# The product with W4 by Strassen's scheme on pairs of 512-token blocks, after all of W3's product

## The chip, the core and the metric

One core of a Trainium2 chip runs the whole program. The metric is the device time of one execution in microseconds (us), as the median of three runs. In the profile, PE is the matmul engine (TensorE), DVE VectorE, ACT ScalarE, POOL GpSimd, and SP the engine that here only issues DMAs. Each engine works through its own instructions in the order in which they stand, and waits at the head of that order.

## The reference

The kernel computes attention over chunks, then two feed-forward layers on 3072 tokens. Only the last one is touched here: x is 3072 x 512, W3 (`w_in`) 512 x 2048, W4 (`w_out`) 2048 x 512.

```python
def _moe2_ref(x, w_in, w_out):
    h = x @ w_in
    g = np.maximum(0.01 * h, h)
    return (g @ w_out).astype(np.float32)
```

The weights arrive in 64-bit floats and are decoded on the chip. Every float32 product is made of three matmuls: each operand is split into a rounded high half and the low rest, and high x high, high x low and low x high are added up in PSUM.

## The kernel before

The first part (attention and the first layer) works on tiles of 128 tokens and leaves x in DRAM (`x2d`) and W3 decoded and split in DRAM (`w3d`). The change leaves it alone. The last layer takes the tokens in six blocks of 512 (`b`) and the 2048 hidden units in 16 slices of 128 (`f`):

- `load_x(b)` fetches a block of x and splits it; `load_w3(f)` fetches a slice of W3, `load_w4(f)` fetches and decodes a slice of W4. Both weights then stay in SBUF.
- `g_unit(b, f, ...)` makes a slice of g, 128 units x 512 tokens, with 12 matmuls into the PSUM tile `gp` (lines 89 and 515 to 529). ACT and DVE turn it into `u`, then the halves `gh` (ACT or DVE) and `gl` (POOL, or DVE in block 0) are made for the next product.
- `o_unit(b, f, ...)` (lines 531 to 548) adds that slice's part of the output with 12 matmuls to four PSUM tiles `po`, one for each 128 tokens, the halves of g being the stationary operand. After the last slice the tiles are copied to `o` (two buffers) and written to `out` in whole rows of 512 floats.

`flush(3)` holds the output's product three slices behind g, so PE alternates: 12 matmuls of line 89, 12 of line 535, 96 times. A scheduler fixes the order on each engine when the program is built. Tiles in a pool with `bufs=n` take turns: the n+1st waits until the first one's readers are done. DMAs also take turns on eight semaphores (shown as DMAHW0 to 7 in the orders below), so at most eight are under way.

Of the kernel before, what the change touches and what calls it, by code (L numbers as in the profile page):

```python
# [9 lines left out]
F32 = mybir.dt.float32  # L10
# [13 lines left out]
LAG = 5  # L24
# [15 lines left out]
def tile_kernel(  # L40
# [33 lines left out]
    w3d = dram.tile([KF2, P, 2 * 512], F32, name="w3d")  # L74

# [390 lines left out]
    sb, sw3 = ExitStack(), ExitStack()  # L466
    w3p = sw3.enter_context(tc.tile_pool(name="w3p", bufs=1, side="right", reuse_waits="tile"))
    NF3 = 8
    w3hl = [w3p.tile([P, NF3, 2, KD, P], F32R, name="w3a")]
    ps_g = sw3.enter_context(tc.tile_pool(name="ps_g", bufs=4, space=PSUM, reuse_waits="tile"))  # L470

    dec2 = sw3.enter_context(tc.tile_pool(name="dec2", bufs=3, side="right", reuse_waits="tile"))

    def load_w3(f):
        w = w3hl[f // NF3][:, f % NF3].bitcast(F32)
        nc.sync.dma_start(out=w.rearrange("p h k f -> p (h k f)"), in_=w3d[f])

    x2e = w3p.tile([P, 2, KD, BT], F32R, name="x2e")
    def load_x(b):
        hl = x2o if b % 2 else x2e  # L480
# [19 lines left out]
    w4p = sb.enter_context(tc.tile_pool(name="w4p", bufs=1, reuse_waits="tile"))  # L500
    w4h = w4p.tile([P, KF2, DM], F32R, name="w4h")
    w4l = w4p.tile([P, KF2, DM], F32R, name="w4l")
    w3hl.append(w4p.tile([P, KF2 - NF3, 2, KD, P], F32R, name="w3b"))
    x2o = w4p.tile([P, 2, KD, BT], F32R, name="x2o")
    pb = sb.enter_context(tc.tile_pool(name="pb", bufs=2, reuse_waits="tile"))
    pg = sb.enter_context(tc.tile_pool(name="pg", bufs=4, reuse_waits="tile"))
    ps_o = sb.enter_context(tc.tile_pool(name="ps_o", bufs=1, space=PSUM, reuse_waits="tile"))

    def load_w4(f):
        decode(load_raw(w4[f * P : (f + 1) * P, :], dec2), w4h[:, f], w4l[:, f], dec2, sub=nc.vector)  # L510

    def g_unit(b, f, xh, xl):
        ps = ps_g.tile([P, BT], F32, name="gp")
        w = w3hl[f // NF3][:, f % NF3]
        wh, wl = w[:, 0], w[:, 1]
        mm3(ps, [((wh[:, kk], wl[:, kk]), (xh[:, kk], xl[:, kk])) for kk in range(KD)])
        u = pg.tile([P, BT], F32, name="u")
        nc.scalar.activation(u, ps, AF.Copy, scale=0.01)  # L518
        nc.vector.tensor_tensor(out=u, in0=ps, in1=u, op=ALU.max)  # L519
        gh = pg.tile([P, BT], F32R, name="gh")  # L520
        gl = pg.tile([P, BT], F32R, name="gl")
        if b == 0:
            nc.scalar.activation(gh, u, AF.Copy)
        else:
            nc.vector.tensor_copy(gh, u)  # L525
        (nc.vector if b == 0 else nc.gpsimd).tensor_tensor(  # L526
            out=gl, in0=u, in1=gh.bitcast(F32), op=ALU.subtract
        )
        return gh, gl

    def o_unit(b, f, gh, gl, po):
        for t in range(TB):
            ts_ = slice(t * P, (t + 1) * P)
            for n, (a, w) in enumerate(((gh, w4h), (gh, w4l), (gl, w4h))):
                nc.tensor.matmul(  # L535
                    po[t], a[:, ts_], w[:, f],
                    start=(f == 0 and n == 0), stop=(f == KF2 - 1 and n == 2),
                )
        if f == KF2 - 1:
            for t in range(TB):  # L540
                late = b == NBLK - 1
                o = pg.tile([P, DM], F32, name="u") if late and t >= 2 else pb.tile([P, DM], F32, name="o")
                od = out[b * BT + t * P : b * BT + (t + 1) * P, :]
                if t % 2:
                    nc.vector.tensor_copy(o, po[t])
                else:
                    nc.scalar.activation(o, po[t], AF.Copy)
# [76 lines left out]
```

## Time and profile before

| | us |
|---|---|
| median of 3 runs (lowest, highest) | 923.99 (921.79, 924.91) |
| profiled execution: span, first to last instruction | 919.1 |
| PE busy in the span | 887.1 (97%) |
| DVE, ACT, POOL busy | 450.9, 315.8, 172.8 |
| share of PE in the chain that ended last | 85% |

The profile shows the span of the profiled execution; a run's time has the launch around it as well, and the median is 4.9 us above this span. Busy time of PE counts matmuls that overlap only once.

### The profile page before, as it was taken

Reading aid. Unit: us, or ns where it says so; the run is one execution under the profiler, and the core shown is the slowest. Engines: PE = TensorE matmul, PEld = TensorE weight load, DVE = VectorE, ACT = ScalarE, POOL = GpSimd, SP = SyncE. Lnnn points to the kernel's source line nnn. Section 1 sums busy time; section 2 is a strip of 40 time slices with the busy share of each in tenths; the row PEclk is TensorE's granted clock in tenths of the full one; section 3 lists DMA queues with packets and bytes.
Section 4 is the critical chain, followed back from the end, with each engine's and each line's share of the span. In section 5 each row is a group of like instructions: output and inputs, shape, how many; then the busy total and the mean of one; then the engine's idle time right before and its main releaser. Section 6 shows DMA issues by size and latency. Waiting matters only on the chain.

```text
span 919.1 us, 13605 instructions
## 1 busy us (share of the span) xinstructions
PE 887.1 (97%) x5248; PEld 713.2 (78%) x5248; DVE 450.9 (49%) x888; ACT 315.8 (34%) x830; POOL 172.8 (19%) x153
## 2 busy tenths in 40 slices
PE   3889999999999989999999999999999999999998
PEld 2467777777777768888888888888888888888886
DVE  4789976676787778389822112211321122112221
ACT  2578854455555555255421112111211121111111
POOL 2233310000000000000022224222422242222221
PEclk9999999999999999999999999999999999999999
DMA  9756785777888764787211001100200110001001
GB/s 230 192 163 185 191 253 172 222 238 201 262 241 251 219 195 172 295 297 267 69 46 46 1 1 46 46 1 1 88 4 1 46 47 1 0 1 46 1 1 46
DMA packets 51504, 109.94 MB, mean 120 GB/s; under 512 B 6640, under 2 KB 23024, under 8 KB 50672
## 3 DMA queue, kind: packets, MB, share of 16 engines
q1 hardware_dynamic: 38480, 93.87, 33.6%
q10 hardware_dynamic: 12960, 15.21, 5.4%
q8 instruction: 41, 0.67, 0.3%
q14 instruction: 23, 0.19, 0.1%
HBM read 79.70 MB, written 29.36 MB: 119 GB/s over the span
## 4 chain that ended last, share of the span: by engine, by line
PE 85%; DVE 7%; DMA 3%; ACT 2%; POOL 1%; issue 1%; SPq 0%; ACTq 0%; DVEq 0%; POOLq 0%
PE po L535 28%; PE gp L89 28%; PE x2p L345 14%; PE h L89 9%; DMA raw<-in_w 2%; PE att L240 2%; PE att L198 1%; DVE so L284 1%; PE tr L254 1%; PE tr L228 1%; ACT p L215 1%; POOL rstd L292 1%; DVE hnm L276 1%; DVE m L122 1%; DVE nms L207 1%
## 5 line engine op out<-in xcount | busy, mean ns | idle before, releaser
L519 DVE TENSOR_TENSOR u<-gp,u 128x512 f32<-128x512 f32 x96 | 66.3, 690 | 324.7 <-ACT u L518 324.7
L518 ACT ACTIVATE u<-gp 128x512 f32<-128x512 f32 x96 | 57.1, 594 | 354.3 <-PE gp L89 354.3
L526 POOL TENSOR_TENSOR gl<-u,gh 128x512 fp32r<-128x512 f32 x80 | 103.2, 1291 | 303.6 <-DVE gh L525 281.7
L535 PE MATMUL po<-w4h,gl 128*128 128x512 f32 x384 | 149.6, 390 | 0.0
L535 PE MATMUL po<-w4l,gh 128*128 128x512 f32 x384 | 149.6, 389 | 0.0
L535 PE MATMUL po<-w4h,gh 128*128 128x512 f32 x384 | 149.5, 389 | 0.0
L345 PE MATMUL x2p<-lhl,w2h 128*128 128x512 f32 x384 | 126.3, 405 | 3.0 <-ACT lhl L333 2.8
L345 PEld LDWEIGHTS x2p<-lhl,w2h 128*128 128x128 f32 x384 | 70.4, 189 | 19.8 <-ACT lhl L333 3.2
L535 PEld LDWEIGHTS po<-w4l,gh 128*128 128x128 f32 x384 | 72.1, 188 | 14.9
L535 PEld LDWEIGHTS po<-w4h,gl 128*128 128x128 f32 x384 | 72.1, 188 | 14.9
L535 PEld LDWEIGHTS po<-w4h,gh 128*128 128x128 f32 x384 | 72.1, 188 | 14.9
L345 PE MATMUL x2p<-lhl,w2l 128*128 128x512 f32 x192 | 77.7, 404 | 0.0
L89 PE MATMUL h<-w1l,xh 128*128 128x512 f32 x168 | 68.0, 405 | 1.9 <-POOL w1l L130 1.9
L89 PE MATMUL h<-w1h,xh 128*128 128x512 f32 x168 | 69.3, 412 | 0.5 <-ACT w1h L129 0.5
L89 PE MATMUL gp<-x2o,w3b 128*128 128x512 f32 x288 | 69.2, 390 | 0.0
L89 PE MATMUL gp<-x2o,w3a 128*128 128x512 f32 x288 | 69.2, 389 | 0.0
L89 PE MATMUL gp<-x2e,w3b 128*128 128x512 f32 x288 | 69.2, 390 | 0.0
L89 PE MATMUL gp<-x2e,w3a 128*128 128x512 f32 x288 | 68.7, 389 | 0.0
L89 PE MATMUL h<-w1h,xl 128*128 128x512 f32 x168 | 66.9, 398 | 0.0
L215 ACT ACTIVATE p<-att,nms 128x64 f32<-128x64 f32 x192 | 57.2, 319 | 22.1 <-DVE nms L208 21.9
L292 POOL TENSOR_TENSOR rstd<-ve,mhalf 128x1 f32<-128x1 f32 x24 | 15.8, 660 | 254.3 <-DVE ve L290 201.6
L89 PEld LDWEIGHTS gp<-x2o,w3b 128*128 128x128 f32 x288 | 54.1, 188 | 11.2
(107 smaller groups left out, 1261.3 us busy)
## 6 DMA issues: line engine op xcount, KB each, us to landing
raw<-in_w SPq DMA_DIRECT2D x48, 512.0 KB, 5.1
kbd<-in_kw SPq DMA_DIRECT2D x46, 256.0 KB, 4.5
vbd<-in_vw SPq DMA_DIRECT2D x46, 256.0 KB, 4.5
lnd<-sl SPq DMA_DIRECT2D x16, 512.0 KB, 3.7
lt<-lnd ACTq DMA_DIRECT2D x64, 128.0 KB, 4.5
q<-in_qt SPq DMA_DIRECT2D x24, 256.0 KB, 4.8
x2d<-x2s ACTq DMA_DIRECT2D x24, 256.0 KB, 3.8
out<-o SPq DMA_DIRECT2D x21, 256.0 KB, 2.0
```

The lines of the kernel that those rows point to most:

```text
L89: nc.tensor.matmul(ps, a, b, start=(i == 0), stop=(i == 3 * n - 1))
L122: nc.vector.scalar_tensor_tensor(out=mu, in0=raw[:, :, 1], scalar=0x80000000, in1=mu, op0=ALU.bitwise_and, op1=ALU.bitwise_or,)
L198: nc.tensor.matmul(sc[cs, 2 * hp : 2 * hp + 2, :], q[:, hp, cs], k[:, :, hp, c, :], start=True, stop=True,)
L207: nc.vector.tensor_reduce(out=nms, in_=sc, op=ALU.max, axis=AX.X, negate=True)
L215: nc.scalar.activation(p[:, h], sc[:, h], AF.Exp, bias=nms[:, h : h + 1], scale=SCALE, accum_out=rs[:, h : h + 1],)
L240: nc.tensor.matmul(xp[cs, 2 * hp : 2 * hp + 2, :], pt[:, hp, cs], v[:, :, hp, c, :], start=True, stop=True,)
L292: nc.gpsimd.tensor_tensor(out=rstd, in0=ve, in1=mhalf, op=ALU.pow)
L345: nc.tensor.matmul(ps, a[:, kk, es], r[:, kk], start=(kk == 0 and n == 0), stop=(kk == KF - 1 and n == 2),)
L518: nc.scalar.activation(u, ps, AF.Copy, scale=0.01)
L519: nc.vector.tensor_tensor(out=u, in0=ps, in1=u, op=ALU.max)
L526: (nc.vector if b == 0 else nc.gpsimd).tensor_tensor(out=gl, in0=u, in1=gh.bitcast(F32), op=ALU.subtract)
L535: nc.tensor.matmul(po[t], a[:, ts_], w[:, f], start=(f == 0 and n == 0), stop=(f == KF2 - 1 and n == 2),)
```

## The change

W4 is cut into a 2 x 2 of blocks: even and odd slices f (1024 units each), and the left and right 256 columns. g is cut likewise into even and odd slices, and block b even and odd of a pair of token blocks `v`. Strassen's scheme gives the four output blocks of a pair from seven products P1 to P7 of sums of these blocks in place of eight. To have a pair's g at hand, W3's product runs first for all six blocks, and g goes to DRAM (`gd`) and comes back.

- `prep_w4` decodes two slices of W4 and forms the seven sums and their halves; they go to DRAM (`w4c`) and come back by `load_w4(r)` into the places of W3 and x as those come free.
- `g_unit` makes u alone, no halves. Pairs of slices are written to `gd`; in odd blocks POOL first forms the difference T3.
- Then each pair `v` runs three stages: `s=0` (P1, P5, P6), `s=1` (P7, P2, P3), `s=2` (P4), each over eight steps p. `load_g` fetches g into the eight tiles of `ring`; `prep_g` forms sums on DVE and splits them (`split`: high half on ACT, low half on DVE), two steps ahead, into nine tiles `h`.
- `product` makes 2 x 3 matmuls; the weights are now the stationary operand, so the output comes out transposed, in three pairs of PSUM tiles A, B and C. After the last step of a product its tiles are combined (`s1`, `u2`, `u3`, `s5`, `y`).
- `put` transposes each finished 128 x 512 tile in blocks of 32 x 32 on DVE into `o` (two buffers) and writes it with four DMAs, two issued by ACT and two by SP, in runs of 32 floats.

```diff
+    w4c = dram.tile([7, P, KF2 // 2, 2, 256], F32, name="w4c")
+    gd = dram.tile([NBLK // 2, 4, P, KF2 // 2, BT], F32, name="gd")
...
+    ring = sl.enter_context(tc.tile_pool(name="ring", bufs=8, reuse_waits="tile"))
...
-        gh = pg.tile([P, BT], F32R, name="gh")
-        gl = pg.tile([P, BT], F32R, name="gl")
...
+        nc.vector.tensor_tensor(out=g[:, f % 2], in0=ps, in1=u, op=ALU.max)
+        if f % 2:
+            k = b % 2
+            if k:
+                nc.gpsimd.tensor_tensor(out=g[:, 0], in0=g[:, 1], in1=g[:, 0], op=ALU.subtract)
+            nc.sync.dma_start(
+                out=gd[b // 2, 2 * k : 2 * k + 2, :, f // 2].rearrange("j q c -> q j c"), in_=g
+            )
...
+    hp = sl.enter_context(tc.tile_pool(name="hp", bufs=9, reuse_waits="tile"))
+    tp = s4.enter_context(tc.tile_pool(name="tp", bufs=2, side="right", reuse_waits="tile"))
...
+    def split(src, lo):
+        h = hp.tile([P, BT], F32R, name="h")
+        nc.scalar.activation(h, src, AF.Copy)
+        nc.vector.tensor_tensor(out=lo, in0=src, in1=h.bitcast(F32), op=ALU.subtract)
+        return h, lo
...
+        if s == 0:
+            tt(out=t2, in0=gf["T3"], in1=gf["B11"], op=ALU.add)
+            t1 = tp.tile([P, BT], F32, name="t1")
+            tt(out=t1, in0=gf["B22"], in1=t2, op=ALU.subtract)
+            return {
+                "P1": split(gf["B11"], g["B11"]),
+                "P5": split(t1, g["B22"]),
+                "P6": split(t2, g["T3"]),
+            }
...
+    def product(r, p, bh, bl, acc):
+        w = w4r[r].rearrange("q (p h c) -> q p h c", p=NPAIR, h=2)
+        for e in range(2):
+            es = slice(e * P, e * P + P)
+            for n, (hl, x) in enumerate(((0, bh), (0, bl), (1, bh))):
+                nc.tensor.matmul(
+                    acc[e], w[:, p, hl, es], x,
...
+    def put(v, i, k, e, y):
+        o = tp.tile([P, 16, 32], F32, name="o")
+        nc.vector.transpose(out=o.rearrange("p b j -> p (b j)"), in_=y)
+        t0 = (2 * v + k) * BT
+        od = out[t0 : t0 + BT].rearrange("(b t) d -> t b d", t=32)
+        for n in range(4):
+            c0 = i * 256 + e * P + 32 * n
+            (nc.sync if n % 2 else nc.scalar).dma_start(
+                out=od[:, :, c0 : c0 + 32], in_=o[32 * n : 32 * n + 32]
+            )
...
+                elif r == "P2":
+                    y = tp.tile([P, BT], F32, name="y")
+                    nc.scalar.activation(y, A[e], AF.Copy)
+                    put(v, 0, 0, e, y)
+                elif r == "P3":
+                    tt(out=u2[e], in0=B[e], in1=u2[e], op=ALU.add)
+                    put(v, 0, 1, e, u2[e])
+                    nc.gpsimd.tensor_tensor(out=u3[e], in0=u3[e], in1=s5[e], op=ALU.add)
+                    put(v, 1, 1, e, u3[e])
+                else:
+                    tt(out=s1[e], in0=C[e], in1=s1[e], op=ALU.add)
+                    put(v, 1, 0, e, s1[e])
```

Three places of the order. First DVE at the end of block 0 before: the copies of two output tiles, the second of which waits for a DMA, as it takes the buffer of an earlier `o`.

```order
L519 TENSOR_TENSOR u_5076<-gp_5063,u_5076 128x512 [waits Activation_49]
L525 CAST gh_5079<-u_5076 128x512 [waits DVE_49,PE_49]
L545 COPY o_5098<-po1_4473 128x512 [waits PE_49]
L545 COPY o_5104<-po3_4475 128x512 [waits DMAHW5_49,DVE_49,PE_49]
L519 TENSOR_TENSOR u_5120<-gp_5107,u_5120 128x512 [waits Activation_49]
```

Now DVE in stage s=2 of the first pair (L678 is the transpose in `put`, L629 the low half of a split, L646 the sum t2 of the next pair, L723 the add of P3).

```order
L678 STREAM_TRANSPOSE o_6815<-y_6813 128x512 [waits Activation_49]
L629 TENSOR_TENSOR h_6873<-t2k_6273,h_6874 128x512 [waits PE_49]
L678 STREAM_TRANSPOSE o_6823<-y_6821 128x512 [waits Activation_49]
L723 TENSOR_TENSOR u20_6335<-B0_6327,u20_6335 128x512 [waits PE_49]
L723 TENSOR_TENSOR u21_6336<-B1_6328,u21_6336 128x512 [waits PE_49]
L646 TENSOR_TENSOR t2k_6273<-ring_6981,ring_6979 128x512 [waits DVE_49]
L678 STREAM_TRANSPOSE o_6836<-u20_6335 128x512 [waits DMAHW6_49,DMAHW5_49,DMAHW7_49,DMAHW0_49,DVE_49]
L629 TENSOR_TENSOR h_6883<-t2k_6273,h_6884 128x512 [waits PE_49,Activation_49]
L678 STREAM_TRANSPOSE o_6843<-u30_6337 128x512 [waits DMAHW3_49,DMAHW2_49,DMAHW4_49,DMAHW1_49,Pool_49]
L678 STREAM_TRANSPOSE o_6850<-u21_6336 128x512 [waits DMAHW6_49,DMAHW5_49,DMAHW7_49,DMAHW0_49,DVE_49]
L678 STREAM_TRANSPOSE o_6857<-u31_6338 128x512 [waits DMAHW2_49,DMAHW3_49,DMAHW1_49,DMAHW4_49,DVE_49,Pool_49]
L629 TENSOR_TENSOR h_6893<-t2k_6273,h_6894 128x512 [waits PE_49,Activation_49]
```

Six transposes share two buffers, so the third to the sixth each wait for four writes of the one two places ahead; the low half of step 5 (h_6893) stands behind the last of them. ACT at the same place issues the writes (L683) and makes the high halves (L628), here of step 4 (h_6884) and step 5 (h_6894):

```order
L628 ACTIVATE h_6884<-t2k_6273 128x512 [waits PE_49]
L683 DMA out_0<-o_6836 32x16x32 [waits DMAHW5_49,DVE_49]
L683 DMA out_0<-o_6836 32x16x32 [waits DMAHW7_49]
L683 DMA out_0<-o_6843 32x16x32 [waits DMAHW1_49,DVE_49]
L683 DMA out_0<-o_6843 32x16x32 [waits DMAHW3_49]
L683 DMA out_0<-o_6850 32x16x32 [waits DMAHW5_49,DVE_49]
L683 DMA out_0<-o_6850 32x16x32 [waits DMAHW7_49]
L683 DMA out_0<-o_6857 32x16x32 [waits DMAHW1_49,DVE_49]
L683 DMA out_0<-o_6857 32x16x32 [waits DMAHW3_49]
L628 ACTIVATE h_6894<-t2k_6273 128x512 [waits PE_49,Activation_49]
```

Before, no high half of ACT stood behind an output write at such a place; now step 5's stands behind the issue of all six tiles' writes. In the third pair step 4's does too. Last, DVE where the stage of g ends and the first pair begins: the sum t1 for P5 stands behind the last `max` (L577).

```order
L577 TENSOR_TENSOR g_6227<-gp_6228,u_6241 128x512 [waits DMAHW6_49,Activation_49,Pool_49]
L577 TENSOR_TENSOR g_6227<-gp_6244,u_6257 128x512 [waits Activation_49]
L648 TENSOR_TENSOR t1_6284<-ring_6281,t2k_6273 128x512
L648 TENSOR_TENSOR t1_6296<-ring_6281,t2k_6273 128x512
L629 TENSOR_TENSOR ring_6281<-t1_6284,h_6289 128x512 [waits Activation_49]
```

Two sums and a low half come after it; before, there was no such place, as the two products alternated to the end.

## Rows read from the trace of the kernel before

**Rows 1.** The core: its span and mean granted clock of PE.

```profile
core 0: 919.1 us, clock 1.000
```

**Rows 2.** Busy time of each engine, share of the span, instructions.

```profile
PE 887.1 (97%) x5248; PEld 713.2 (78%) x5248; DVE 450.9 (49%) x888; ACT 315.8 (34%) x830; POOL 172.8 (19%) x153
```

**Rows 3.** The chain that ended last: shares by engine and by line.

```profile
PE 85%; DVE 7%; DMA 3%; ACT 2%; POOL 1%; issue 1%; SPq 0%; ACTq 0%; DVEq 0%; POOLq 0%
PE po L535 28%; PE gp L89 28%; PE x2p L345 14%; PE h L89 9%; DMA raw<-in_w 2%; PE att L240 2%; PE att L198 1%; DVE so L284 1%; PE tr L254 1%; PE tr L228 1%; ACT p L215 1%; POOL rstd L292 1%; DVE hnm L276 1%; DVE m L122 1%; DVE nms L207 1%
```

**Rows 4.** The same chain in order of time: start us, us, what.

```profile
393.10 10.88 PE gp L89 x48
403.98 2.72 PE po L535 x12
...
409.42 2.72 PE po L535 x12
...
904.46 10.89 PE po L535 x48
```

**Rows 5.** Two stretches: us, busy per engine (count), granted clock, DMA share, GB/s.

```profile
400.00:420.00 20.00, 20.00 (x90) 16.58 (x89) 19.87 (x39) 12.49 (x23) 0.00 (x0) 1.00 0.88 325
...
600.00:700.00 100.00, 100.00 (x443) 82.85 (x442) 23.21 (x40) 14.55 (x25) 28.57 (x23) 1.00 0.06 22
```

**Rows 6.** Groups by line and shape: busy us, mean ns | idle before, releaser.

```profile
L316 DVE STREAM_TRANSPOSE sl<-so 128x512 f32<-128x512 f32 x32 | 21.4, 692 | 0.3
...
L526 DVE TENSOR_TENSOR gl<-u,gh 128x512 fp32r<-128x512 f32 x16 | 11.0, 687 | 5.7 <-ACT gh L523 5.6
...
L523 ACT ACTIVATE gh<-u 128x512 fp32r<-128x512 f32 x16 | 10.1, 629 | 5.9 <-DVE u L519 5.8
...
L526 POOL TENSOR_TENSOR gl<-u,gh 128x512 fp32r<-128x512 f32 x80 | 103.2, 1291 | 303.6 <-DVE gh L525 281.7
```

**Rows 7.** Timeline from 396 us: start us, us, instruction; pairs merged.

```profile
398.42 1.14 ACT L129 ACTIVATE w4h<-m 128x512 fp32r<-128x512 f32 x2
...
400.08 1.28 DVE L130 TENSOR_TENSOR w4l<-m,w4h 128x512 fp32r<-128x512 f32 x2
```

**Rows 8.** Timeline of DVE at the end of block 0; in brackets its idle time.

```profile
487.44 0.68 DVE L545 COPY o<-po 128x512 f32<-128x512 f32 x1
490.26 0.69 DVE L545 COPY o<-po 128x512 f32<-128x512 f32 x1 [2.13 <-DMA out<-o]
```

**Rows 9.** Timeline of the end.

```profile
914.01 0.37 ACTq L548 DMA_DIRECT2D out<-o  x1
...
914.95 0.39 PE L535 MATMUL po<-w4h,gl 128*128 128x512 f32 x1
...
915.44 0.69 DVE L545 COPY u<-po 128x512 f32<-128x512 f32 x1 [0.74 <-PE po L535]
916.16 0.33 SPq L548 DMA_DIRECT2D out<-u  x1
```

**Rows 10.** DMA from 574 to 582 us (four output tiles), queue line: share of 16 engines.

```profile
DMA packets 576, 1.05 MB, mean 131 GB/s; under 512 B 64, under 2 KB 64, under 8 KB 576
...
q1 hardware_dynamic: 576, 1.05, 33.9%
```

**Rows 11.** DMA from 26 to 29 us, with 4-byte loads.

```profile
DMA packets 1066, 0.95 MB, mean 318 GB/s; under 512 B 785, under 2 KB 785, under 8 KB 1066
...
q1 hardware_dynamic: 1066, 0.95, 109.7%
```

**Rows 12.** Loads of 512 KB in 128 packets (line 95): issue ns; landing us.

```profile
L95 SPq DMA_DIRECT2D raw<-in_w x32: 327/333/4987, 2.4 to 443.8; - x32
...
DMA to landing us min/median/max: 3.3/5.5/12.4
```

**Rows 13.** Loads of 512 KB in 512 packets (line 97).

```profile
L97 SPq DMA_DIRECT2D raw<-in_w x16: 378/384/392, 109.7 to 353.5; - x16
...
DMA to landing us min/median/max: 3.6/4.5/8.2
```

More of the change, by code (lines that the diff above doesn't have):

```diff
@@ L517, in g_unit @@
[L517 removed]
+        w = w3r[f].rearrange("p (h k f) -> p h k f", h=2, k=KD)
+        mm3(ps, [((w[:, 0, kk], w[:, 1, kk]), (xh[:, kk], xl[:, kk])) for kk in range(KD)])
+        u = g3.tile([P, BT], F32, name="u", bufs=3)
         nc.scalar.activation(u, ps, AF.Copy, scale=0.01)
[L519 to L525 removed]
@@ L526, in g_unit @@
[L526 to L547, printed above, removed]
-                (nc.scalar if late and t % 2 == 0 else nc.sync).dma_start(out=od, in_=o)
@@ L572, in tile_kernel @@
+            for _ in range(2 if b else 1):
+                next(prep, None)
             if f == 8 and b + 1 < NBLK:
                 nx = load_x(b + 1)
-    flush(0)
-    sb.close()
-    sw3.close()
+            if b == NBLK - 1 and f in (5, 11):
+                load_w4({5: "P6", 11: "P7"}[f])
+        if b == NBLK - 2:
+            for _ in prep:
+                pass
+            sd.close()
+            load_w4("P1")
+            load_w4("P5")
+    hp = sl.enter_context(tc.tile_pool(name="hp", bufs=9, reuse_waits="tile"))
@@ new lines, in put @@
+    def put(v, i, k, e, y):
[7 more added lines that the diff above has]
+                out=od[:, :, c0 : c0 + 32], in_=o[32 * n : 32 * n + 32]
+            )
+    steps = [(v, s, p) for v in range(NBLK // 2) for s in range(3) for p in range(NPAIR)]
@@ new lines, in tile_kernel @@
+    AHEAD = 2
+    halves = {}
+    for n in range(AHEAD):
+        halves[n] = prep_g(*steps[n])
+    tt = nc.vector.tensor_tensor
+    for n, (v, s, p) in enumerate(steps):
+        if n + AHEAD < len(steps):
+            halves[n + AHEAD] = prep_g(*steps[n + AHEAD])
+        x = halves.pop(n)
+        if s == 0 and p == 0:
+            A, B, C = (
+                [pool.tile([P, BT], F32, name=f"{c}{e}") for e in range(2)]
+                for c, pool in (("A", ps_ab), ("B", ps_ab), ("C", ps_c))
+            )
+            s1, s5, u2, u3 = ([tp.tile([P, BT], F32, name=f"{c}{e}", bufs=1) for e in range(2)] for c in ("s1", "s5", "u2", "u3"))
+        order = {0: ("P1", "P5", "P6"), 1: ("P7", "P2", "P3") if p else ("P2", "P3", "P7"), 2: ("P4",)}[s]
+        for r in order:
+            acc = {"P1": A, "P2": A, "P5": B, "P3": B}.get(r, C)
+            product(r, p, *x[r], acc)
+            if p < NPAIR - 1:
+                continue
+            for e in range(2):
+                if r == "P1":
+                    nc.scalar.activation(s1[e], A[e], AF.Copy)
+                elif r == "P5":
+                    nc.scalar.activation(s5[e], B[e], AF.Copy)
+                elif r == "P6":
+                    tt(out=u2[e], in0=C[e], in1=s1[e], op=ALU.add)
+                elif r == "P7":
+                    tt(out=u3[e], in0=C[e], in1=s1[e], op=ALU.add)
+                elif r == "P2":
[10 more added lines that the diff above has]
+                    put(v, 1, 0, e, s1[e])
@@ L579 @@
+    s4.close()
+    sl.close()
+    sr.close()
 def kernel(**inputs):
```

157 lines of the change are left out of this document (117 added, 40 removed).

## The prediction

> **What bounds the kernel now.** I read the clock first: 1.000 over the span [rows 1], so every matmul runs at the higher level, 2.4 GHz. PE is busy 97% of the span, DVE 49%, ACT 34% [rows 2]. Busy PE alone would not prove a bound, so I read the chain that ended last: PE holds 85% of it, lines 535 and 89 have 28% each [rows 3]. In order of time the last layer is one unbroken string of PE work, from 393.10 us to 904.46 + 10.89 = 915.35 us [rows 4]. That is 522.25 us for 96 x 24 = 2304 matmuls, 0.2267 us each; two pieces of line 535 with 12 of line 89 between them begin 5.44 us apart, which is 24 of these [rows 4]. In the middle of it DVE is busy 23%, ACT 15% and the DMAs 6% [rows 5]: the stage is bound by the number of matmuls and has room beside it. Here a matmul less is 0.2267 us less, as long as PE is fed.
>
> I count from the profiled execution's span, 919.1 us [rows 1]. Its own total time is not on the page; the median of the runs, 923.99, is 4.9 us above the span, and I keep these 4.9 us for what lies around it.
>
> **What is removed.** W4's product takes 7/8 of 1152 matmuls: 144 go, 144 x 0.2267 = 32.6 us. W3's keeps its 1152.
>
> **What costs nothing in the stage of g, and why.** A unit of 12 matmuls lasts 2.72 us [rows 4], and ACT and DVE each spend about 0.6 us on u. The decoding and the seven sums of W4 are 8 x 14 = 112 operations of DVE, at 0.69 us [rows 6] 77 us over the first four blocks of 43.5 us, beside 96 x 0.69 = 66 us for u: under the 261 us of the stage. With that cover gone those 77 us would be on the path. The tightest stretch is block 0, where W3 must come twice as fast as before: its second half 4.2 MB, g 3.7, x 1.0, W4 and its sums 2.8, in 40 us 290 GB/s, where the trace shows 325 GB/s at a DMA share of 0.88 [rows 5]. I take no stall, with up to 3 us for the range. The stage ends at 393.1 + 1152 x 0.2267 = 654.3 us.
>
> **What the pairs need.** A pair has 336 matmuls, 76.2 us. DVE has 96 operations of 128 x 512 in it (72 sums and low halves of steps 0 to 15, 8 of P4, 8 adds, 8 transposes). One lasts 687 to 692 ns [rows 6], but the next starts 0.60 us after it (two take 1.28 us [rows 7]), so 58 us; ACT's copies are 0.63 us [rows 6] at a step of 0.52 [rows 7], some 62 of them, 33 us. Both fit. A step of s=0 asks DVE for 5 x 0.60 = 3.0 of its 4.08 us. Reading g back is 12.6 MB in the two long stages, 193 GB/s, again under rows 5's 325. So PE should run freely except at three places.
>
> **First place: from g to the first pair.** Behind the last matmul of g stand ACT's copy (0.6), the last max (0.7), then t1 (0.65), its high half (0.63) and low half (0.7), by [rows 6]: about 3.4 us. P1 covers 1.36 us of it. I take 2.0 us.
>
> **Second place: the output of a pair.** This decides the sum. In s=2 PE needs a new split every 6 x 0.2267 = 1.36 us, from ACT and DVE in order. On DVE six transposes share two buffers of `o`, so each from the third on waits until the four writes of the one two places ahead have landed; ACT issues half of these writes itself, and in the first two pairs the high half for step 5 stands behind the last issue (step 4 in the third pair).
>
> How long do four writes take? Before, a copy waited 2.13 us for one whole write of 256 KB [rows 8]. Its transfer is a quarter of 33.9% x 16 x 8 us = 43.4 us of engine time [rows 10], over 16 engines 0.68 us, so 1.45 us are fixed. In the new form the same 256 KB are 2048 packets of 128 bytes, 128 on each engine. No row has a 128-byte write. From below: if only bytes counted, 43.4 us for 1.05 MB gives 5 ns, and the wait stays about 2.1 us. From above: 43.4 us over 576 packets is 75 ns each. In between, a load of 512 packets lands 0.3 us later than one of 128 at its fastest, 3.6 against 3.3 us [rows 12, 13], for 24 more packets on each engine: 12.5 ns a packet, with bytes 17. And from 26 to 29 us 785 small packets ran among 281 large ones: 109.7% x 16 x 3 = 52.7 us, less 0.95 MB at the rate above (39.3 us), leaves 17 ns each [rows 11]. A share over 100% says that these times are stretched by company, so I take 15 ns: 1.92 us of transfer for a tile, 1.45 + 1.92 = 3.37 us for its writes.
>
> Now walk the engines, with zero at the end of P3. ACT makes step 3's high half to 0.7, y of both halves to 1.2 and 1.7. DVE: first transpose 1.25 to 1.95, landed 5.3; second to 3.15, landed 7.25 (behind the first on the same engines); adds and a sum to 4.9; third 5.35 to 6.05, landed 9.4; fourth 7.3 to 8.0, landed 11.4; fifth at 9.45; sixth 11.45 to 12.15. ACT issues its two writes (0.37 each [rows 9]) to 12.9 and makes the high half of step 5 to 13.5; DVE's low half is ready at 14.2, and PE starts step 5 at 14.0 instead of 5 x 1.36 = 6.8. That is 7.2 us in each of the first two pairs. In the third, step 4 starts at 14.0 instead of 5.4: 8.6 us. Together 23.0 us. What is late next, the splits of the next pair, is ready by then, about 0.6 us apart, and its P6 needs C only 2.7 us after P4. By the same walk a packet at 5 ns gives 15.9 us, at 12 ns 19.5, at 20 ns 29.7, at 30 ns 45.2.
>
> **Third place: the end.** Before, 919.1 - 915.35 = 3.75 us lay behind the last matmul [rows 4], a copy, an issue and a write [rows 9]. Now two adds and two transposes to 2.2, four writes 3.4, and the 0.6 that lay behind the landing: 6.2. Cost 2.4 us (1.2 at 5 ns, 4.4 at 30).
>
> **Sum.** -32.6 + 2.0 + 23.0 + 2.4 = -5.2 us: a span of 913.9, a median of 918.8 us, 0.6% less. Some 0.3% is what a measurement of this kernel can tell from no change.
>
> **The rivals.**
> *The writes don't hurt:* bytes count and not packets. For it: four times the packets landed only 0.3 us later at best [rows 12, 13]. -32.6 + 2.0 + 15.9 + 1.2 = -13.5, so 910.5 us. It can't be better than this, as 2.13 us for a write is measured [rows 8].
> *A 128-byte write costs twice a small load's packet, 30 ns:* these are writes to DRAM in short runs, which the trace does not have. The sum is -32.6 + 2.0 + 45.2 + 4.4 = +19, 943 us, slower. It decides from about 18 to 19 ns upwards, where the stalls eat the 32.6 us. Against it: the middle prices above come from loads under company and are, if anything, too high.
> The Trainium skill speaks for this rival: its page DMA: Bandwidth & Descriptors, section Specifications, gives 512 B as the smallest transfer for full rate and says that below it the DMA engine does read-modify-write. By that rule each of the 49152 runs of the output would be handled twice. No row here shows it or speaks against it.
> *Another wait takes over:* g comes back late (the third `ring` tile of a group is asked for only when PE has left the step before, some 8 us ahead, and loads landed in 3.3 to 12.4 us [rows 12]), or DVE's splits wait for ACT's one by one (3 x 0.6 more on 3.0 us is 4.8 against 4.08 in the 24 steps of s=0, 17 us). For it: three of W4's seven blocks share the queue with g at the start of the pairs. Against it: the order interleaves two steps, and the DMA share was 6% there. +10 to +25 on my sum: 929 to 944.
> *No gain because PE is not the bound:* against rows 3 and 4; not counted.
>
> **How the numbers follow.** My forecast, a packet at 12 to 20 ns: -9 to +2 us, 915 to 926, chance 0.42; writes without harm: 0.18; 30 ns or more: 0.27; another wait: 0.13. Of the first, what ends below 921.2 is 0.26, and what ends between 921.2 and 926.8 is 0.16. Faster is 0.26 + 0.18 = 0.44; slower is most of the last two, 0.38; the rest, 0.18, is no change that can be told. The range leaves out the upper part of the dear writes and a little at the bottom: 908 to 943. For the forecast alone it is 915 to 926.
>
> **What would show it.** The matmuls of W4 should number 1008, and the pieces of s=0 and s=1 run without gaps, 32.6 us each. In s=2 PE should stop once, at step 5, 5 and 4, for 7, 7 and 9 us, with DVE's transposes (line 678) waiting for `out<-o`. `out<-o` in 64 KB should land some 2 to 3 us after issue. The prediction is wrong if the transposes do not wait; if the landing is far over 3 us; if PE has gaps in s=0 or s=1 on `ring`; or if the stage of g ends later than 657 us.

## The result, and the profile after

The changed kernel takes 934.25 us (median of 4 runs, 930.68 to 936.94), the kernel before 924.18 (4 runs, 921.79 to 924.91): a ratio of 1.0119, with a 95% interval of 1.0082 to 1.0155. It is 1.2% slower where 0.6% faster was forecast. The profiled execution took 936.94 us. That is 1.7 us above its span, so of the 4.9 us that the forecast kept for what lies around the span some 3 us were scatter between executions; the forecast difference of 0.6% doesn't depend on it. Its core row, to set beside [rows 1], and from its page PE's busy time [rows 2] and the row of the granted clock over 40 slices:

```profile
core 0: 935.2 us, clock 0.982
```

```profile
PE 871.3 (93%) x5104; PEld 692.5 (74%) x5104; DVE 608.3 (65%) x1100; ACT 408.6 (44%) x988; POOL 112.8 (12%) x103
...
PEclk9999999999999999999999999999899989989997
```

The 144 matmuls are gone (5248 to 5104), but PE's share fell from 97 to 93%, and the clock, 1.000 before, has dips. The chain in order of time [rows 4] says where (columns: start us, us, what):

```profile
639.81 26.08 PE gp L91 x115
...
672.68 2.56 PE C L669 x6
675.24 1.96 PE A L669 x6
677.19 1.36 PE B L669 x6
...
736.85 5.40 DMA out<-o
...
742.37 0.72 DVE o L678
...
743.11 0.37 ACTq L683
...
743.52 2.54 DMA out<-o
...
746.19 0.72 DVE o L678
...
746.94 0.37 ACTq L683
...
747.35 2.44 DMA out<-o
749.79 0.62 ACT h L628
...
750.46 6.57 PE C L669 x18
757.03 1.36 PE A L669 x6
...
836.79 6.11 PE C L669 x18
...
919.00 8.28 PE C L669 x21
```

W3's stage ends at 665.7 us, not at 654.3. Six matmuls of a pair take 1.36 us, as forecast, except at four places: at the start of the first pair, and behind each output, where a chain of landings (`out<-o`), transposes (`o`) and issues (ACTq) stands and 18 matmuls then take 6 us and more. The windows of the stage of g, and three short ones (columns: stretch, length, busy of PE, PEld, DVE, ACT, POOL with counts, granted clock, DMA share, GB/s):

```profile
393.00:436.50 43.50, 43.50 (x194) 36.03 (x193) 22.14 (x38) 15.94 (x27) 0.00 (x0) 1.00 0.95 329
436.50:480.00 43.50, 41.62 (x182) 33.46 (x180) 30.37 (x47) 15.28 (x26) 12.76 (x9) 1.00 0.81 278
480.00:524.00 44.00, 41.48 (x177) 32.48 (x176) 32.74 (x51) 18.92 (x32) 10.05 (x7) 1.00 0.85 298
524.00:567.50 43.50, 41.87 (x184) 33.94 (x182) 28.45 (x45) 16.15 (x28) 12.21 (x8) 1.00 0.87 306
567.50:611.00 43.50, 43.34 (x191) 35.91 (x192) 13.48 (x21) 11.65 (x20) 10.16 (x8) 1.00 0.42 158
...
672.00:675.00 3.00, 3.00 (x8) 2.31 (x7) 3.00 (x6) 1.84 (x4) 0.00 (x0) 0.50 0.89 332
...
750.40:754.00 3.60, 3.54 (x8) 2.52 (x9) 3.56 (x6) 3.31 (x8) 0.00 (x0) 0.50 0.83 180
...
757.00:760.00 3.00, 3.00 (x15) 2.49 (x14) 3.00 (x6) 1.62 (x3) 0.00 (x0) 1.00 0.15 26
```

Block 0, which I had called the tightest, has no gap (43.50 of 43.50). The three blocks behind it lose some 2 us each while the DMAs have room. And behind a stop the granted clock is 0.50, the lower of its two levels (1.2 GHz): 8 matmuls in 3.6 us instead of 15 in 3.0.

What waited for what from 436 to 570 us (us in total, times, longest):

```profile
ACT mh L549 <- DVE mm L543: 29.4, 7, 7.2
ACT mm L523 <- DMA raw<-in_w: 26.8, 6, 8.0
...
PEld gp L91 <- DVE g L577: 10.7, 11, 2.1
...
DVE t2k L646 <- DMA w4c<-mm: 7.2, 1, 7.2
```

ACT stands at the head of its order up to 8.0 us for a raw block of W4, or up to 7.2 us for DVE's part of the decoding; `u` of g stands behind, its PSUM buffer stays full, and PE waits. The timeline at the output of the first pair, to set beside the walk of the prediction:

```profile
736.40 3.10 ACTq L683 DMA_DIRECT2D out<-o  x4
...
742.37 0.71 DVE L678 STREAM_TRANSPOSE o<-u 128x512 f32<-128x512 f32 x1 [2.06 <-DMA out<-o]
...
743.11 6.56 ACTq L683 DMA_DIRECT2D out<-o  x8
...
749.77 1.67 ACT L628 ACTIVATE h<-t2k 128x512 fp32r<-128x512 f32 x3 [9.59 <-DMA out<-o]
...
750.46 1.95 PE L669 MATMUL C<-h,ml 128*128 128x512 f32 x3 [5.55 <-ACT h L628]
```

The transposes wait, ACT issues eight writes in a string for 6.56 us, and the copy `h` for PE's next step stands behind it. ACT's string is paced by the transposes here: in the chain above it issues a write 0.02 us behind the end of one, and each of them waits for the landing of an earlier write. The first landing took 5.40 us, with loads of g on the DMA engines beside it, the later two 2.54 and 2.44. Landing, and the DMA queues from 744 to 749 us:

```profile
DMA to landing us min/median/max: 1.9/2.5/5.5
```

```profile
DMA packets 5932, 0.75 MB, mean 149 GB/s; under 512 B 5931, under 2 KB 5931, under 8 KB 5931
...
q1 hardware_dynamic: 3108, 0.39, 47.3%
q10 hardware_dynamic: 2823, 0.35, 42.6%
```

A 128-byte packet takes 89.9% x 16 x 5 us / 5931 = 12.1 ns.

The end [rows 9]:

```profile
928.61 1.29 DVE L678 STREAM_TRANSPOSE o<-s 128x512 f32<-128x512 f32 x2
929.34 1.97 SPq L683 DMA_DIRECT2D out<-o  x4
```

The difference of the spans, part by part. The two spans differ by 16.1 us, the medians of the runs by 10.1 only: the profiled execution before was faster than its four timed runs (its span is 919.1, and 921.79 us less 1.7 is 920.1), and the one after is the slowest of its four. So some 6 us of the measured column are scatter between executions; the later start holds 2.0 of them, and where the rest lies is not shown. A stop is the time from one matmul's start to the next, less 0.2267 us:

| part | forecast, us | measured, us | from |
|---|---|---|---|
| 144 matmuls fewer | -32.6 | -32.6 | 0.2267 each |
| start of the last layer | 0 | +2.0 | 395.1 against 393.1; untouched work, 390.0 to 397.2 in the runs below |
| stage of g | 0 | +9.4 | 395.1 to 665.7, less 261.2 |
| stops: start of the first pair | +2.0 | +2.9 | 1.48 + 1.39 |
| stops: outputs | +23.0 | +22.5 | 7.5 + 8.6 + 6.4 |
| matmuls at the lower clock in the pairs | not a term | +8.3 | 665.7 to 928.0, less 1008 x 0.2267 and the stops |
| end | +2.4 | +3.5 | 935.2 - 928.0, less 3.75 |
| sum | -5.2 | +16.0 | spans 919.1 and 935.2: +16.1 |

### The profile page after: what moved, and what is told of

It reads as the page before. It is cut to its first block, busy times and chain, and to the rows that moved or that the text cites. A ratio compares the mean times of both kernels' runs of the same rounds, so it can differ in the third digit from the quotient of the medians.

```text
span 935.2 us, 14252 instructions
## 1 busy us (share of the span) xinstructions
PE 871.3 (93%) x5104; PEld 692.5 (74%) x5104; DVE 608.3 (65%) x1100; ACT 408.6 (44%) x988; POOL 112.8 (12%) x103
## 5 line engine op out<-in xcount | busy, mean ns | idle before, releaser
L577 DVE TENSOR_TENSOR g<-gp,u 128x512 f32<-128x512 f32 x96 | 64.9, 687 | 103.1 <-ACT u L576 102.3
L347 PEld LDWEIGHTS x2p<-lhl,w2h 128*128 128x128 f32 x384 | 70.9, 190 | 19.2 <-ACT lhl L335 2.3
L628 ACT ACTIVATE h<-ring 128x512 fp32r<-128x512 f32 x96 | 57.4, 625 | 52.4 <-DMA ring<-gd 33.9
L629 DVE TENSOR_TENSOR ring<-ring,h 128x512 fp32r<-128x512 f32 x96 | 62.1, 685 | 23.7 <-ACT h L628 23.7
L91 PE MATMUL gp<-ml 128*128 128x512 f32 x288 | 67.3, 391 | 2.2 <-DVE g L577 2.2
L91 PE MATMUL gp<-mr 128*128 128x512 f32 x288 | 66.5, 390 | 1.5 <-DVE g L577 1.5
L91 PE MATMUL gp<-ml,mr 128*128 128x512 f32 x288 | 66.1, 390 | 1.7 <-DVE g L577 1.7
L669 PE MATMUL A<-h,ml 128*128 128x512 f32 x192 | 67.3, 392 | 0.0
L669 PE MATMUL C<-h,mr 128*128 128x512 f32 x192 | 67.3, 394 | 0.0
L91 PE MATMUL gp<-mr,ml 128*128 128x512 f32 x288 | 66.3, 390 | 0.8 <-DVE g L577 0.8
L91 PEld LDWEIGHTS gp<-ml 128*128 128x128 f32 x288 | 53.7, 188 | 15.4 <-DVE g L577 4.4
L91 PEld LDWEIGHTS gp<-ml,mr 128*128 128x128 f32 x288 | 53.9, 188 | 13.4 <-DVE g L577 2.1
```

The costliest lines, as they stand in the source:

```text
L91: nc.tensor.matmul(ps, a, b, start=(i == 0), stop=(i == 3 * n - 1))
L347: nc.tensor.matmul(ps, a[:, kk, es], r[:, kk], start=(kk == 0 and n == 0), stop=(kk == KF - 1 and n == 2),)
L577: nc.vector.tensor_tensor(out=g[:, f % 2], in0=ps, in1=u, op=ALU.max)
L628: nc.scalar.activation(h, src, AF.Copy)
L629: nc.vector.tensor_tensor(out=lo, in0=src, in1=h.bitcast(F32), op=ALU.subtract)
L669: nc.tensor.matmul(acc[e], w[:, p, hl, es], x, start=(r in FIRST and p == 0 and n == 0), stop=(p == NPAIR - 1 and n == 2), skip_group_chec ...
```

## The experiments

Each profiled run by its parts, in us, from the starts of the first matmul of g, the first and the last of the pairs, and its span. The label names the run in the text; a run is compared by its parts, since the start scatters. Each is one profiled execution. Where an edit leaves a part alone, the part still differs: the stage of g from 268.6 to 270.6 us in seven runs, the pairs from 260.2 to 261.9 in four. So a difference of 2 us in one part says little, and the stage of g lost 7.4 to 9.4 us. The expectations count the stops of the change a little wider, as 7.8, 8.8 and 6.6 us.

| run | start of g | stage of g | pairs | end | span |
|---|---|---|---|---|---|
| the change | 395.1 | 270.6 | 261.9 | 7.6 | 935.2 |
| o_sp | 395.2 | 268.7 | 247.8 | 15.1 | 926.8 |
| o_sh | 395.5 | 269.6 | 262.1 | 7.6 | 934.8 |
| g_nodec | 394.2 | 261.1 | 260.2 | 8.0 | 923.5 |
| g_noload | 390.0 | 267.5 | 260.4 | 7.4 | 925.3 |
| o_pool | 394.5 | 278.8 | 234.7 | 14.8 | 922.8 |
| o_wide | 391.3 | 269.6 | 237.2 | 6.7 | 904.9 |
| g_ahead | 394.0 | 265.9 | 260.7 | 7.6 | 928.2 |
| g_late | 397.2 | 266.7 | 263.9 | 7.6 | 935.4 |
| fill | 393.1 | 270.4 | 256.6 | 7.5 | 927.6 |
| best0 | 393.9 | 264.8 | 251.1 | 15.2 | 925.0 |
| best1 | 391.4 | 263.4 | 254.9 | 15.4 | 925.0 |
| best2 | 393.7 | 265.4 | 235.9 | 15.4 | 910.4 |
| wide_ord | 392.8 | 268.6 | 255.3 | 6.7 | 923.4 |
| defer | 395.4 | 270.1 | 243.3 | 7.5 | 916.3 |
| best3 | 395.1 | 263.8 | 245.5 | 7.5 | 911.9 |

PE's own work is 261.2 us in the stage of g and 228.5 in the pairs.

### The outputs: buffers or ACT's queue

**o_sp**, all writes on SP:

```diff
-            (nc.sync if n % 2 else nc.scalar).dma_start(
+            nc.sync.dma_start(
```

> All four writes of a transposed tile are issued by SP, none by ACT; the two buffers of `o` stay. Theory (the buffers of `o` hold DVE, and ACT's issues only add to it): the transposes still wait for the writes of the tile two places ahead, which now leave one queue 0.35 us apart, so PE still stops 4 to 8 us at each output, 23 us in all become 14 to 24, and the span stays between 925 and 937 us. Rival (ACT's queue is what holds the splits of P4, the buffers hardly matter): the stops fall under 2 us each, the clock stays at 1.000 there, and the span is 905 to 915 us.

The three stops in the third step are gone: no gap there is over 0.5 us, although the transposes still wait for landings, 14.3 us in all. The stops went with ACT's writes, as the rival had it; but the compiler also moved DVE's low halves of step 4 to 7 ahead of the third transpose (736.10 to 739 us against 740.90), so this run alone doesn't tell ACT's order from DVE's. And a new stop of 5.9 us comes at the start of the second and third pair, and here is why (timeline; brackets: idle before and its releaser):

```profile
733.04 26.04 SPq L683 DMA_DIRECT2D out<-o  x32
759.18 3.83 SPq L622 DMA_DIRECT2D ring<-gd  x7
```

```profile
763.80 1.29 DVE L646 TENSOR_TENSOR t2k<-ring 128x512 f32<-128x512 f32 x2 [6.85 <-DMA ring<-gd]
```

SP has 32 writes in one string, and the loads that the next pair needs stand behind them. The span lies in the theory's range, but by another mechanism than the theory's.

**o_sh**, more buffers, ACT still issuing (`t1` and `y` take the same name and count):

```diff
-        o = tp.tile([P, 16, 32], F32, name="o")
+        o = tp.tile([P, 16, 32], F32, name="t1", bufs=6)
```

> The tiles `t1`, `y` and `o` share six buffers instead of two each; ACT keeps issuing half the writes. Theory (buffers of `o`): no transpose waits for a landing any more, the stops of PE in the third step of a pair fall from 7.8, 8.8 and 6.6 us to under 1.5 us each, and with the clock that comes back there (some 8 us) the span is 903 to 914 us. Rival (the 128-byte packets themselves are the limit, 2048 of them a tile): more buffers only move the wait to the next queue, the stops stay above 4 us each, and the span is 922 us or more.

No transpose waits any more, and the stops at the outputs stay: 6.1, 6.3 and 4.5 us, 5.6 less in all. The pairs win nothing, because a new stop of 8.75 us comes at the start of the first pair, where the change has 1.39: DVE waits at the next sum `t1` until a write of g has landed, with the low half that PE needs behind it. In the change the sum has no such wait; presumably the six shared buffers lie where g was:

```profile
DVE t L648 <- DMA gd<-g: 8.1, 1, 8.1
```

So the buffers were worth some 5.6 us, and the span hides it. What is left at the outputs is ACT. Its timeline:

```profile
742.27 10.42 ACTq L683 DMA_DIRECT2D out<-t  x12
752.74 2.19 ACT L628 ACTIVATE h<-t2k 128x512 fp32r<-128x512 f32 x4 [10.57 <-DMA out<-t]
```

With the buffers free the compiler puts twelve writes in a string where there were eight, and they take 10.42 us. The issues alone take 0.35 us each (median); in between ACT waits. In the compiled order of ACT shown with the change, its writes wait for DMAHW5, 7, 1 and 3 in turn, and then for 5 again. In this run's trace ACT stands likewise at one of four semaphores in turn before its writes.

So a write goes out only when ACT's fourth write before it has landed, whatever `o` has of buffers: in the change the buffers set the pace, and with more of them these semaphores do. Landings of 3 us (median) for each four writes of twelve are about the 10.4 us.

**o_pool**, o_sp and the loads of `ring` on POOL's queue:

```diff
-            nc.sync.dma_start(out=t.bitcast(F32), in_=gd[v, BLK[n], :, 2 * q : 2 * q + 2])
+            nc.gpsimd.dma_start(out=t.bitcast(F32), in_=gd[v, BLK[n], :, 2 * q : 2 * q + 2])
```

> All writes of the output are issued by SP, and the loads of `ring` move to POOL's queue, so that no load stands behind a write. Theory (in the third step of a pair it is queues that cost: first ACT's, and when SP has all the writes, the loads behind them): the stops of 6.1 us at the start of the second and third pair go too, no gap of PE over 2 us is left behind 670 us, and the span is 8 to 13 us shorter than that of the run with all writes on SP (926.8 us): 914 to 919 us. Rival (the loads were late because the DMA engines were full of 128-byte packets): the gaps stay at 4 us or more, and the span is 922 us or more.

The pairs come down to 234.7 us, 6 above PE's own work, without a gap over 1 us but for the first start: the queues were it. But POOL also makes differences of g in the stage of g, and the first pair's loads now stand among them. The waits from 436 to 570 us:

```profile
POOL ring L622 <- DMA gd<-g: 21.6, 3, 11.0
```

The stage of g became 8.2 us longer, which put the span, 922.8, at the rival's figure, for a reason that is not the rival's.

### The form of the writes, or their place

**o_wide** (the transposed place in the output is left out):

```diff
...
-                out=od[:, :, c0 : c0 + 32], in_=o[32 * n : 32 * n + 32]
+                out=out[r0 : r0 + 32], in_=o[32 * n : 32 * n + 32].rearrange("p b j -> p (b j)")
```

> The same 96 writes of 64 KB from the same engines, but each goes to 32 whole rows of 2 KB instead of 512 pieces of 128 bytes: the transposed place of the output is left out, bytes, issues and buffers stay. Theory (ACT stands behind its issues, each of which waits until the write with the same completion semaphore, four of ACT's before, has landed; the form of the packets counts only by the landing): a write lands in 1.9 to 2.2 us instead of 2.5, and the three stops fall from 7.8, 8.8 and 6.6 us to 4 to 6 us each. Rival (128 bytes are what costs): the stops fall under 2.5 us each, and the span is 15 us or more shorter than 935.2.

The stops fall to 1.8, 1.6 and none, the pairs to 237.2 us. The rival's numbers came out. But the compiler had also put copies between ACT's writes (timeline of ACT; why it did is not shown):

```profile
736.50 2.65 ACTq L682 DMA_DIRECT2D out<-o  x4
...
739.25 0.63 ACT L628 ACTIVATE h<-t2k 128x512 fp32r<-128x512 f32 x1 [4.00 <-DMA out<-o]
```

**wide_ord** keeps the whole rows (the same part is left out) and puts the copies back behind the string of eight:

```diff
...
+            if s2 == 2 and p2 == (5 if v2 < NBLK // 2 - 1 else 4):
+                with tc.issue_after(sent[0].ins):
+                    halves[n + AHEAD] = prep_g(v2, s2, p2)
```

> Whole rows of 2 KB as in the earlier run (the transposed place of the output is left out), but ACT's copies of the third step may only stand behind the last of its eight writes in a string, as in the change. Theory (the place of ACT's writes makes the stops, the form only their length): the stops come back, 3 to 6 us each where the change has 7.8, 8.8 and 6.6, and the span is 912 to 924 us. Rival (the form alone does it: a row lands so much sooner that the order doesn't matter): the stops stay under 2.5 us each as in the earlier run with whole rows, span 903 to 910 us.

```profile
735.48 6.29 ACTq L682 DMA_DIRECT2D out<-o  x8
741.87 1.67 ACT L628 ACTIVATE h<-t2k 128x512 fp32r<-128x512 f32 x3 [7.84 <-DMA out<-o]
```

The stops are back: 6.9, 7.2 and 5.1 us, a little more than the theory gave, where the change has 7.5, 8.6 and 6.4. In one order the form of the packets is worth 22.5 - 19.2 = 3.3 us of stops; the order on ACT is worth the rest, 19.2 against 3.4 in o_wide.

**defer** is the other cross: 128-byte writes, four in a string.

```diff
+        if s == 2 and p in (3, 5):
+            with tc.issue_after(last_h[0].ins):
+                for a in held[:2]:
+                    put(*a)
...
-                    put(v, 0, 1, e, u2[e])
+                    held.insert(e, (v, 0, 1, e, u2[e]))
```

> The change with its 128-byte writes, its two buffers of `o` and both queues; only the four transposes and writes behind P3 are handed out later, two at step 3 and two at step 5 of the third step, behind the copies made there, so that ACT has four writes in a string and not eight. Nothing is left out. Theory (the place of ACT's writes): the stops fall from 7.8, 8.8 and 6.6 us to under 3 us each, the clock stays up, and the span is 908 to 918 us. Rival (the 128-byte form): each string of four writes still takes ACT some 5 us in which PE runs dry, the stops stay 5 us or more, cut in two pieces, span 925 us or more.

The stops are 1.8 and 4.1 us at the first two outputs and none at the third, another 1.3 and 1.4 at the start of the next pair, and the pairs take 243.3 us, 18.6 less. One of the three is over the theory's 3 us, and behind it the clock fell to 0.50 for some matmuls, which the theory had not; the rest fits it. Set crosswise, the pairs as a whole lose 18.6 us by the order with 128-byte writes (261.9 against 243.3) and 18.1 with whole rows (255.3 against 237.2), and 6.6 or 6.1 us by the form. The order of defer is near that of o_wide, not the same.

### The stage of g

**g_nodec** (decoding, sums and halves of W4 are left out; loads and writes stay, from a tile of zeros):

```diff
-            nc.scalar.activation(df, r.bitcast(F32)[:, :, :, 1], AF.Abs, scale=65536.0)
...
-        nc.sync.dma_start(out=dst[0], in_=h.bitcast(F32))
+        nc.sync.dma_start(out=dst[0], in_=mm0)
```

> The decoding of W4, its sums and halves on ACT and DVE are left out; its loads and writes stay, the writes take their data from one tile of zeros. Theory (the stage of g loses its 11 us because decoding operations that wait stand ahead of the copies and the maxima of g on ACT and DVE): PE has no gap over 0.3 us before the last block and the last product of W3 ends at 653 to 656 us. Rival (the DMA engines, 0.81 to 0.95 busy in that stage, bring x, W3 and W4 too slowly): it ends at 661 us or later, with the gaps at about the same places.

```profile
436.50:480.00 43.50, 43.50 (x194) 36.03 (x193) 10.99 (x17) 11.76 (x20) 14.08 (x11) 1.00 0.94 319
480.00:524.00 44.00, 44.00 (x196) 36.45 (x195) 11.16 (x17) 11.65 (x20) 6.36 (x5) 1.00 0.97 341
```

PE has no gap, while the DMAs are busier than before (0.94 and 0.97). The stage takes 261.1 us, PE's own work. So x and W3 come in time, and all of the loss hangs on the decoding on ACT and DVE. The run leaves out the decoding's work together with its waits for raw blocks, and can't tell these two apart.

**g_noload** (14 of 16 raw loads are left out; first diff) and **g_ahead** (raw blocks a pair ahead; second):

```diff
-            raw = dec2.tile([P, 512, 2], U32, name="raw4")
...
+            raw = raw0[j]
```

```diff
...
-            raw = dec2.tile([P, 512, 2], U32, name="raw4")
-            f = 2 * p + j
-            nc.sync.dma_start(out=raw.rearrange("p f w -> p (f w)"), in_=w4[f * P : (f + 1) * P, :])
+            raw = raws.pop(0)
+            load_raw4(2 * p + j + 2)
```

> Only the first two blocks of raw W4 are loaded, and each decoding step reads them again: 14 of 16 loads are left out, the decoding and all its writes stay. Theory (the decoding stands still because raw W4 comes late, ACT 27 us in all): the stage of g ends at 654 to 658 us. Rival (the decoding itself is too much in one place, copies of 1.06 and 0.85 us on ACT and sums of 1.2 and 0.95 us on DVE in front of the copy and the maximum of a unit): it ends at 661 us or later.

> The raw blocks of W4 get four buffers instead of two, and each is loaded one pair of blocks ahead. Nothing is left out. Theory (ACT and DVE stand before u and the maxima while a decoding step waits for its raw block): the gaps of PE between 455 and 525 us fall from about 7 us in all to under 3, the stage of g ends at 656 to 660 us. Rival (the decoding's own copies and sums are too much in one place): as in the run with 14 loads left out, 5 us of gaps stay there and only what lies at 562 to 568 us goes: 659 to 662 us; or, if it only moves the work forward into the first block, the stage ends no earlier than 663.

Without late raw blocks the stage still takes 267.5 us, 3.1 less than the change and 1.1 less than the fastest run that left it alone. So the late loads are 1 to 3 us of the loss, and most of it is the decoding's own operations in front of a unit's copy and maximum. With four buffers the stage takes 265.9; but from 436 to 570 us ACT still waited 23.2 us for raw blocks, against 26.8 before, so what gave these 4.7 us isn't shown. g_noload ended 8.2 us earlier (657.5 us), and 5.1 of these are its start at 390.0: the theory's range was met by luck.

**g_late** holds the first pair's sums behind the last maximum:

```diff
...
+    with tc.issue_after(last[0].ins):
+        for n in range(AHEAD):
+            halves[n] = prep_g(*steps[n])
```

> The sums, copies and halves of the first pair may stand on DVE only behind the last maximum of g; before, five of the sums of line 646 stood among the maxima. Nothing is left out. Theory (the first of them holds DVE for 7.2 us until the last write of W4's halves has landed): the gaps at 562 and 566 us, 2.1 us in all, go, and those at 455 to 525 us stay, so the stage of g ends at 663 to 664 us; the first pair then starts later by the sums that were done early, 0.6 us for one. Rival (DVE isn't what PE waits for there): the gaps at 560 to 570 us stay at 2 us.

The gaps at 562 and 566 us go and the stage is 3.9 us shorter, but the first pair now stops 4.0 us for the low half of its first step, and the pairs take 2.0 more. The span is what it was because this run also began 2.1 us later. About half of the stage's gain comes back in the pairs.

### The clock

**fill** adds 24 matmuls that nothing reads at each stop:

```diff
...
+            for _ in range(24):
+                tc.keep_in_program_order(
+                    nc.tensor.matmul(D, w[:, 0:P], w[:, 0:BT], start=True, stop=True)
+                )
```

> Where PE stops in the third step of a pair, 24 matmuls of 128 x 512 on resident data go into a free PSUM tile that nothing reads, 72 in all, 16.3 us of work that the computation doesn't need. Theory (the waits at the outputs cost twice: once as waits, once because the granted clock falls behind them, 0.85 to 0.89 in those stretches): PE has work in the wait, the clock stays at 1.000 from 735 us on, the matmuls behind the stops take 0.227 us again, and the span is 5 to 9 us shorter than 935.2: 926 to 930 us. Rival (the lower clock there costs next to nothing, since ACT and DVE set the pace in that step anyway): the span stays within 2 us of 935.2, or grows.

```profile
743.00:747.00 4.00, 3.82 (x18) 2.85 (x16) 1.08 (x3) 0.76 (x2) 0.00 (x0) 1.00 0.73 121
747.00:751.00 4.00, 3.78 (x16) 2.87 (x17) 4.00 (x7) 4.00 (x9) 0.00 (x0) 1.00 0.67 157
```

With 72 more matmuls the pairs take 5.3 us less. At the first and third output the clock stays up; at the second a stop of 1.9 us is left, and some 9 slower matmuls behind it, most of them the added ones. The rest of the span's 7.6 us is the earlier start.

### Putting it together

**best0** is g_ahead, all writes on SP, and on POOL the first three groups of loads of the second and third pair; **best1** also spreads the decoding:

```diff
+        eng = nc.gpsimd if v and s == 0 and q < 3 else nc.sync
...
-            for _ in range(2 if b else 1):
+            for _ in range(2 if b and f % 2 else 1):
```

> Three edits of the runs before together: raw W4 one pair ahead in four buffers; all writes of the output on SP; the loads of `ring` for the first six tiles' steps of the second and third pair on POOL, all others on SP as in the change. Nothing is left out. Theory (the causes found are separate and add up): 5.3 us from the stage of g, no stop over 2 us in the pairs and the clock back there, 935.2 - 6 - 23 = 904 to 908 us of span. Rival (the edits give each other's gain back: earlier raw blocks or POOL's loads bring a new wait in the stage of g, as POOL's loads did): 914 us or more, with a gap over 3 us between 455 and 700 us.

> The same three edits, and W4's decoding spread thinner: from the second block on three steps for two units of g instead of four. Theory (the 4 us of gaps left between 475 and 513 us come from too many decoding operations in front of one unit's copy and maximum): those gaps fall under 2 us, and the span is 2 to 3 us shorter than that of the run with three edits. Rival (the compiler's order decides what stands where, and not the rate at which the program hands the steps out): the same gaps in another place, within 1.5 us of that run.

Both rivals' spans were nearer. The fourth group of loads, left on SP, was late behind the writes: gaps of 4.2 and 2.4 us at 764, 4.0 and 2.2 at 850. The spreading gave 1.4 us in the stage of g, and an earlier start 2.5; the pairs took 3.8 more with stops less than 1 us longer, mostly because the clock was at 0.50 for longer.

**best2** moves those loads too; **best3** is the diffs of defer and g_ahead and the spreading, and no more.

```diff
-        eng = nc.gpsimd if v and s == 0 and q < 3 else nc.sync
+        eng = nc.gpsimd if v or s else nc.sync
```

> The edits of the run before, but all loads of `ring` except those of the first step of the first pair go through POOL; in that run the fourth group of loads of a pair was still on SP, behind the writes, and PE stopped there for 7 us at 764 and 851 us. Nothing is left out. Theory (a load behind a write is the last of the stops): both stops go, and from the first stop of the first pair (655.9 us in the run before) it goes on as in the run with all loads on POOL, which took 248.4 us from there to its end: a span of 902 to 908 us, faster than both kernels, ratio to the kernel before 0.980 to 0.990. Rival (the loads are late because the 128-byte packets fill the DMA engines while a pair's output goes out, whatever the queue): the stops stay over 3 us each, and the span is 915 us or more.

> The run before and the two edits of the stage of g (raw W4 one pair ahead in four buffers; decoding spread thinner), with no load on POOL and both queues for the writes. Nothing is left out. Theory (the two causes add up, and the end of the last pair keeps both queues, where the run with writes on SP alone and loads on POOL took 15 us behind its last matmul): a span of 898 to 908 us, ratio to the kernel before 0.975 to 0.988. Rival (without its own queue the loads of g wait behind the writes again): stops of 4 us or more at the start of the second and third pair, span 912 us or more.

best2 takes 910.85 us (906.19 to 912.13), ratio to the kernel before 0.9853, interval 0.9822 to 0.9885; best3 909.96 us (906.89 to 913.71), 0.9844, interval 0.9815 to 0.9873. Both are some 1.5% faster than the kernel before, and the intervals stay clear of 1; none of their runs is as slow as the fastest of the change, 930.68. The profiled spans miss their ranges by 2.4 and 3.9 us: best2's first pair began 4.3 us later than the run that its range was taken from (a start 2.3 us later, a stage of g 2.0 us longer), and best3 keeps stops of 1 to 1.5 us at the first two outputs. In both cases the profiled execution was also the slowest of the kernel's runs. best2 has the better pairs, best3 the better end, since SP alone takes 15.4 us there and two queues 7.5.

## Why the prediction was wrong

- **What is removed** was right: 1008 matmuls of W4 at 0.2267 us.
- **"What costs nothing in the stage of g" failed**: the overlap that it put at nothing cost 9.4 us (7.4 in the fastest run with this stage unchanged) where at most 3 were allowed. It weighed sums, 77 us of decoding and 66 of maxima under 261, and DMA bandwidth in block 0. g_nodec shows that x and W3 came in time and that the decoding, with its waits for raw blocks, was all of it. The gaps lie where a decoding operation that waits for a load, or for its neighbour on the other engine, stands at the head of an in-order engine with g behind it, and there are four PSUM buffers of cover. The total can't show this. The text named the line at which it would be wrong, 657 us; it ended at 665.7, of which 2.0 us are the later start.
- **The clock was not in the sum**, 8.3 us in the pairs. Rows 1 showed 1.000 for a kernel whose PE never stopped; the forecast of three stops of 7 to 9 us should have carried a price for what follows them. The rows give it: 0.50 behind each of the three outputs. fill shows that it comes from the idle PE, since work that nobody needs took it away at two of three places.
- **The second place was right in mechanism, and in size partly by luck**: 22.5 us against 23.0, with transposes that wait for landings and ACT's writes in front of the copies. But its packet price, 15 ns, was above the 12.1 measured, and by its own walk 12 ns gives 19.5. The walk had a tile's writes land after 3.4 to 4.1 us; in the first pair the first landing took 5.40 and the later ones 2.5. The stops were 7.5, 8.6 and 6.4 us where 7.2, 7.2 and 8.6 were said, so the third pair came out lower and the second higher. The Trainium skill's page DMA: Bandwidth & Descriptors, section Specifications, has the engine read, modify and write below 512 B. No run here shows whether it does; 12.1 ns is near the 12.5 that the prediction worked out for loads, and not twice that. The rival at 30 ns falls, though the kernel was slower.
- **The rival "writes don't hurt"** was called the best case, 15.9 us of stops. In the change's order whole rows leave 19.2, and in o_wide's order 3.4. But the walk took the order on ACT as given, and o_wide and defer show that the order is most of the cost.
- **The first place** was 2.9 us, not 2.0; **the end** 3.5, not 2.4. In s=0 and s=1 PE ran without gaps, as said.

The sum -5.2 missed +16.1 by 21.3 us: 9.4 from the stage of g, 8.3 from the clock, 2.0 from a start that scatters, 1.5 from the small terms. Against the medians, +10.1, the miss is 15.3 us. The stated range, 908 to 943, holds 934.25, but by luck: its upper part was kept for dear packets and for waits in the pairs on g or on the splits, and neither came. What stays open is why the start of g differs by up to 7 us between runs of the same first part, and how the rest of the stage's loss divides between ACT's copies and DVE's sums.

## What to carry to other kernels

When work is laid "beside" a stage, its total busy time says nothing by itself: read which operation stands at the head of each in-order engine, what it waits for, and how many buffers cover whoever stands behind. Writes issued by an engine that also feeds PE are part of its compute order, and where they stand can cost far more than their form; moving them to another queue helps only if no load stands behind them there. A forecast that has PE idle for some 6 us should also price the matmuls behind the stop.

## What was not expected of the hardware

- Behind stops of 5.5 to 6.7 us, and behind the two of 1.48 and 1.39 us at 667 us, which have one matmul between them, the granted clock was 0.50, and the next 6 to 14 matmuls began some 0.43 us apart. Behind single stops of up to 1.8 us in the stage of g it stayed at 1.00. The small stops don't settle it: the same two at the start of the first pair were followed by 1.00 in o_sp, o_pool and best0, and in fill the clock fell behind a single one of 1.9 us. The Trainium skill's page TensorE: Matmul & The Clock Gate, Part 1, says that activity releases the clock and idling throttles it to half; the rows of the long stops agree, with 0.50 and 1.00.
- 72 matmuls that nobody needs made the pairs 5.3 us shorter.
- Writes of 128 bytes to DRAM went at 12.1 ns a packet and engine, near the 12.5 ns worked out for loads from rows 12 and 13.
